# Rounding the weights of an attention and FFN kernel through PSUM, in the score buffers

## The chip, the cores and the metric

The kernel runs on one core of a Trainium2 chip. The metric is the device time of one execution in microseconds, given as the median of several runs. Engines are named as the profile names them: PE (TensorE matmuls), PEld (its weight loads), DVE (VectorE), ACT (ScalarE), POOL (GpSimd), SP (SyncE, which issues most DMAs here). Each engine has a queue of its own.

## What is computed

Two blocks follow each other. Routing attention: queries and keys are each assigned to the nearest of 16 centroids of their head, and a query sees only keys with the same assignment. Then a feed-forward block with a quick GELU. The attention inputs are float32; the two weight matrices arrive as float64 words, and the kernel rounds them to float32 itself, from their integer halves.

```python
batch, n_heads, seq, head_dim = (4, 8, 768, 64); n_clusters = 16
n_tokens, d_model, d_ff = (3072, 512, 2048)
...
q_assign = np.argmax(np.einsum('bhsd,hcd->bhsc', q_n, c_n), axis=-1)
k_assign = np.argmax(np.einsum('bhsd,hcd->bhsc', k_n, c_n), axis=-1)
mask = q_assign[:, :, :, None] == k_assign[:, :, None, :]
scores = scale * np.matmul(q, k.transpose(0, 1, 3, 2))
scores = np.where(mask, scores, -1000000000.0)
...
attn = attn / (np.sum(attn, axis=-1, keepdims=True) + 1e-09)
attn_out = np.matmul(attn, v)
...
x = attn_out.transpose(0, 2, 1, 3).reshape(B * S, H * D)
h = x @ w_in
g = h * (1.0 / (1.0 + np.exp(-1.702 * h)))
return g @ w_out
```

## The kernel before

The work is cut into units. A pair p is two heads of one batch (16 pairs). A group g is one pair and one half of its 768 queries (32 groups), and a unit u is a group and one tile of 128 keys (six to a group, 192 units). A unit's scores are two matmuls into one buffer of the PSUM pool ps_s (L386). For the pairs of batch 0 (p < HP) the mask is added in PSUM by two small matmuls over one-hot codes (part, L400), and the exponential goes to SBUF (L411, tile A). For later pairs the exponential is written back to PSUM and DVE multiplies it by the mask (L422). POOL adds up the exponentials of a group's key tiles (sum, L432), PE multiplies by v (values, L443), and after a group's six tiles `normalise` forms the row sums on PE (L455), takes the reciprocal and the product on DVE (L458, L460), which gives x. `check` (L470, L472) lets ACT sum the reciprocals for a test at the end; its result `bad` decides whether a slower general path is run after all. It is read into every engine by values_load.

The main loop runs over turns t of two units each, and its text is the order of each engine's queue: the schedule is manual. A turn issues the scores, part and exponentials of both units, a step of the weight rounding, the masks and sums, the values of the turn before, `normalise` when a group is done, the preparation of later pairs (prep_turn, prep_near, prep_assign, prep_hot, prep_spread), the check, and then chunks of the FFN. The first turns (t < TB = 24) belong to batch 0. When four groups are normalised, `ffn_chunks` appends 28 chunks: 16 of the first layer (`first`, L489 with tanh L494 and the product L496) and 12 of the second (`second`, L506, L512). The first group of four is complete in turn 13. `rate` chunks are owed per turn, 28 / 11.5 = 2.43. Chunks call `round_to`, which rounds on demand whatever weights they need.

The weights are rounded in 32 pieces of 128 x 512, first w_in's and then w_out's. SP loads a piece into one of three tiles raw (L146). `split_w` takes the exponent and the high mantissa bits (L159, L161 on DVE) and rescales both on ACT (L163, L165). `join_w` puts the sign in (L171), adds the low mantissa word (L174), both on DVE, and multiplies the two parts on POOL (L177). `round_next` splits piece i and joins piece i - 1. It is called once ahead of the loop and once a turn, and twice a turn from t = 12 (TB // 2).

PSUM: ps_s has two buffers of two banks (scores), ps_o one bank (values), ps_m three banks (everything else, the FFN too).

Of the kernel before, what the change touches and what calls it, by code (L numbers as in the profile page):

```python
# [8 lines left out]
FP32 = mybir.dt.float32  # L9
# [29 lines left out]
def fast(  # L39
# [26 lines left out]
    P = 128  # L66
# [74 lines left out]
    w_raw, w_pow = {}, {}  # L141
# [12 lines left out]
    def split_w(i):  # L154

        hi = w_raw[i][:, :, 1]
        w = w_chunks[i][0]
        e = wp.tile([P, WN], I32, name="e")
        nc.vector.tensor_scalar(out=e, in0=hi, scalar1=EXP, scalar2=None,  # L159
                                op0=ALU.bitwise_and)  # L160
        nc.vector.tensor_scalar(out=w.bitcast(I32), in0=hi, scalar1=0xFFFFF,  # L161
                                scalar2=None, op0=ALU.bitwise_and)
        nc.scalar.activation(out=e, in_=e, func=AF.Relu, scale=8.0,  # L163
                             bias=low[:, 0:1])
        nc.scalar.activation(out=w, in_=w.bitcast(I32), func=AF.Copy,  # L165
                             scale=2.0 ** -20, bias=1.0)
        w_pow[i] = e

    def join_w(i):
        raw, e, w = w_raw.pop(i), w_pow.pop(i), w_chunks[i][0]  # L170
        nc.vector.scalar_tensor_tensor(  # L171
            out=e, in0=raw[:, :, 1], scalar=-2 ** 31, in1=e,
            op0=ALU.bitwise_and, op1=ALU.bitwise_or)
        nc.vector.scalar_tensor_tensor(  # L174
            out=w, in0=raw.bitcast(U32)[:, :, 0], scalar=2.0 ** -52, in1=w,
            op0=ALU.mult, op1=ALU.add)
        nc.gpsimd.tensor_tensor(out=w, in0=w, in1=e.bitcast(FP32),  # L177
                                op=ALU.mult)

    w_done = [0]  # L180

    def round_next():
        i = w_done[0]
        if i < NW:
            load_w(i + 2)
            split_w(i)
        if 0 < i <= NW:
            join_w(i - 1)
        w_done[0] += 1

    def round_to(n):
        while w_done[0] <= min(n, NW):
            round_next()
# [333 lines left out]

    prep_at = {}
# [14 lines left out]
    def prep(p, i):  # L543
        if i == 0 and p:
            load_v(p)
        PREP[i](p)
        if i in (1, 3) and loads:
            load_qk(*loads.popleft())

    rate = (NF + NH * (NF // 4)) / (TB / 2 - 0.5)  # L550
# [3 lines left out]
    round_next()  # L554
    for t in range(NT + 2):
        us = range(2 * t, 2 * t + 2) if t < NT else ()
        for u in us:
            scores(u)
        if t == 0:
            prep(0, 6)  # L560
        for u in us:
            part(u)
        for u in us:
            exps(u)
        round_next()
        for u in us:
            mask(u)
        work = sorted(prep_at.get(t, ()), key=lambda w: PREP[w[1]] != prep_near)
        while work and PREP[work[0][1]] == prep_near:
            prep(*work.pop(0))  # L570
        if 1 <= t <= NT:
            for u in range(2 * t - 2, 2 * t):
                values(u)
        owed = owed + rate if ffn else 0.0
        if t >= 2 and (t - 2) % TG == TG - 1:
            normalise((t - 2) // TG)
        for p, i in work:
            prep(p, i)
        if recs:
            check(*recs)  # L580
        if t >= TB // 2:
            round_next()
        while owed >= 1 and ffn:
            ffn.popleft()()
            owed -= 1

# [15 lines left out]
    is_bad = nc.values_load(bad[0:1, 0:1], min_val=0, max_val=1)  # L602
    while ffn:
        ffn.popleft()()
    return is_bad
# [440 lines left out]
```

## Time and profile before

| | |
|---|---|
| median of 3 runs | 1090.87 us (1090.25 to 1093.47) |
| the profiled execution | 1093.03 us, span 1091.2 us |
| mean granted TensorE clock | 0.987 |
| PE busy | 1050.7 us (96%) |
| DVE busy | 484.9 us (44%) |
| ACT busy | 355.2 us (33%) |
| POOL busy | 336.6 us (31%), of it L432 292.8 and L177 43.2 |

The span is the time from the first to the last instruction. Busy shares are means over a span whose stages differ, so the stretches matter more than the means. A row of a timeline gives the start, the duration, the engine, the line and the operation with its operands, and in brackets how long the engine stood idle ahead of it and what ended that. An x with a number is a count of merged instructions; an fp32 matmul of this kernel leaves two records. In the table by stretch each engine's busy time is followed by its count of instructions, and the last three columns are the granted clock (1.00 is full speed), the share of the DMA engines and the GB/s they moved.

### The profile page before, as it was taken

To read this page: it belongs to the slowest core of one execution; us is meant where nothing else is said; L and a number is where in the kernel's file an instruction comes from. 1 tells how busy PE (TensorE), PEld (TensorE's weight loads), DVE (VectorE), ACT (ScalarE), POOL (GpSimd) and SP (SyncE) were. 2 spreads that over 40 slices of the span, in tenths; PEclk is the share of its full clock that TensorE was granted. 3 is DMA by queue.
4 is the path that set the end of the run, shared out by engine and by line. 5 is a ranking of instruction groups with operands and counts; after the bars stand their busy time and mean duration, and the time that the engine had idled before them with its cause. 6 is when DMAs were issued, how large, how long until landed. Compare 5 with 4: busy or idle time off the path is not lost. (4 is left out here: it accounts for less than half of the span.)

```text
span 1091.2 us, 10473 instructions
## 1 busy us (share of the span) xinstructions
PE 1050.7 (96%) x3982; PEld 494.2 (45%) x3982; DVE 484.9 (44%) x712; ACT 355.2 (33%) x665; POOL 336.6 (31%) x200
## 2 busy tenths in 40 slices
PE   6787899999999999999999999999999999999997
PEld 3332454445544455445554455444554445444543
DVE  4889986125442444424443254332553144421100
ACT  5564554233322333223432233322431132311100
POOL 2677646213232333122231243123233233320000
PEclk9898899999999999999999999999999999999999
DMA  8543442110100010101200001020000000000000
GB/s 232 154 127 105 130 112 73 46 49 20 46 23 27 10 29 15 31 25 54 51 22 17 20 15 27 3 70 10 8 8 11 10 11 1 1 10 20 1 10 22
DMA packets 64811, 45.12 MB, mean 41 GB/s; under 512 B 51952, under 2 KB 57584, under 8 KB 64752
## 3 DMA queue, kind: packets, MB, share of 16 engines
q1 hardware_dynamic: 64608, 44.33, 14.5%
q8 instruction: 33, 0.54, 0.2%
q14 instruction: 26, 0.21, 0.1%
q10 hardware_dynamic: 144, 0.03, 0.0%
HBM read 38.04 MB, written 6.31 MB: 41 GB/s over the span
## 5 line engine op out<-in xcount | busy, mean ns | idle before, releaser
L489 PE MATMUL m<-x,w_in 128*128 128x384 f32 x1024 | 346.8, 494 | 7.7 <-DVE g L496 3.1
L432 POOL TENSOR_TENSOR sum<-sum,A 128x768 f32<-128x768 f32 x128 | 234.4, 1831 | 383.5 <-DVE A L422 364.2
L506 PE MATMUL m<-w_out,g 128*128 128x512 f32 x768 | 337.7, 594 | 0.0
L422 DVE SCALAR_TENSOR_TENSOR A<-qb,code,s 128x384 f32<-128x384 uint8 x288 | 157.6, 610 | 274.6 <-ACT s L411 251.5
L489 PEld LDWEIGHTS m<-x,w_in 128*128 128x128 f32 x1024 | 192.3, 192 | 146.8 <-issue 16.0
L506 PEld LDWEIGHTS m<-w_out,g 128*128 128x128 f32 x768 | 143.4, 190 | 174.6 <-issue 171.7
L496 DVE SCALAR_TENSOR_TENSOR g<-g,m 128x384 f32<-128x384 f32 x128 | 70.1, 553 | 228.6 <-ACT g L494 228.4
L386 PE MATMUL s<-T,T 64*128 64x384 f32 x768 | 154.7, 522 | 4.4 <-ACT A L411 4.4
L411 ACT ACTIVATE s<-s 128x768 f32<-128x768 f32 x144 | 107.9, 793 | 136.1 <-PE s L386 136.1
L443 PE MATMUL o<-A,inv 128*64 128x384 f32 x768 | 145.9, 501 | 0.0
L494 ACT ACTIVATE g<-m 128x384 f32<-128x384 f32 x128 | 61.6, 486 | 203.3 <-PE m L489 203.1
L432 POOL TENSOR_TENSOR sum<-A 128x768 f32<-128x768 f32 x32 | 58.4, 1826 | 180.0 <-DVE A L422 179.2
L386 PEld LDWEIGHTS s<-T,T 64*128 64x128 f32 x768 | 67.2, 190 | 87.3 <-issue 52.7
L458 DVE RECIPROCAL short<-m 128x384 f32<-128x384 f32 x32 | 81.7, 2553 | 27.2 <-PE m L455 27.2
L443 PEld LDWEIGHTS o<-A,inv 128*64 128x64 f32 x768 | 46.9, 137 | 85.3 <-issue 85.0
L512 ACT ACTIVATE y<-m 128x512 f32<-128x512 f32 x24 | 14.2, 593 | 155.9 <-PE m L506 142.7
L470 ACT ACTIVATE short<-short 128x384 f32<-128x384 f32 x32 | 16.7, 523 | 103.6 <-DVE x L460 103.6
L411 ACT ACTIVATE A<-s 128x768 f32<-128x768 f32 x48 | 36.4, 808 | 33.0 <-PE s L400 32.8
L269 ACT COPY T<-m 128x384 f32<-128x384 f32 x64 | 29.9, 480 | 41.6 <-PE m L264 41.4
L264 PE MATMUL m<-ident,in 128*128 128x128 f32 x192 | 34.7, 302 | 8.4 <-DVE short L458 3.5
L264 PEld LDWEIGHTS m<-ident,in 128*128 128x128 f32 x192 | 22.0, 149 | 28.1 <-issue 11.1
L177 POOL TENSOR_TENSOR w_in<-w_in,e 128x512 f32<-128x512 f32 x16 | 21.0, 1313 | 42.5 <-DVE w_in L174 42.5
(68 smaller groups left out, 412.4 us busy)
## 6 DMA issues: line engine op xcount, KB each, us to landing
raw<-in_moe_w_in_dram SPq DMA_DIRECT2D x16, 512.0 KB
raw<-in_moe_w_out_dram SPq DMA_DIRECT2D x16, 512.0 KB
in<-in_q_dram SPq DMA_DIRECT2D x32, 192.0 KB
in<-in_k_dram SPq DMA_DIRECT2D x32, 192.0 KB
inv<-in_v_dram SPq DMA_DIRECT2D x16, 384.0 KB
out_dram<-y SPq DMA_DIRECT2D x24, 256.0 KB
qb<-line SPq DMA_DIRECT2D x12, 192.0 KB
line<-row SPq DMA_DIRECT2D x12, 1.5 KB
```

Source lines behind the costliest of these rows:

```text
L264: nc.tensor.transpose(out=ps[:, n * P:(n + 1) * P], in_=qk_in[p, w][:, h * NH + n].rearrange("p a d -> p (a d)"), identity=ident)
L269: nc.scalar.copy(dst, ps[:, 0:HALF])
L386: nc.tensor.matmul(out=ps[:, a, 0:HALF], lhsT=T[p, 1][rows, kt * P:(kt + 1) * P], rhs=T[p, 0][rows, h * HALF:(h + 1) * HALF], start=True, ...
L411: nc.scalar.activation(out=A_of[u] if p < HP else s, in_=s, func=AF.Exp, scale=SCALE)
L422: nc.vector.scalar_tensor_tensor(out=A_of[u][:, a, :], in0=qcode[p][:, a, h * HALF:(h + 1) * HALF], scalar=code[p][:, kt % NH, 1, kt // NH ...
L432: nc.gpsimd.tensor_tensor(out=sum_of[g], in0=A_of[u - 1] if kt == 1 else sum_of[g], in1=A, op=ALU.add)
L443: nc.tensor.matmul(out=o_of[g][a * D:(a + 1) * D, 0:HALF], lhsT=v_in[p][:, a, kt, :], rhs=A[:, a, :], start=(kt == 0), stop=(kt == NJ - 1))
L458: nc.vector.reciprocal(out=rec, in_=ps[:, 0:HALF])
L489: nc.tensor.matmul(out=ps[:, 0:HALF], lhsT=w_in[:, c, f * P:(f + 1) * P], rhs=xT[c], start=(c == 0), stop=(c == NCH - 1))
L494: nc.scalar.activation(out=g, in_=ps[:, 0:HALF], func=AF.Tanh, scale=0.851)
L496: nc.vector.scalar_tensor_tensor(out=g, in0=g, scalar=1.0, in1=ps[:, 0:HALF], op0=ALU.add, op1=ALU.mult)
L506: nc.tensor.matmul(out=ps[:, 0:DM], lhsT=hs[f][:, n * P:(n + 1) * P], rhs=w_out[:, f, :], start=(f == 0), stop=(f == NF - 1))
```

## The change

The multiply that POOL did for each piece moves to DVE. The two rescaled parts are no longer kept in SBUF (e and the weight tile) but in a tile r taken from ps_s, the pool of the score buffers: ACT writes both parts there, and DVE reads them from there, with the result of L174 written to PSUM too. `round_next` becomes `begin` (load, split) and `finish` (join); a piece is begun and finished inside one turn. In the turns of batch 0 the two units of a turn are issued one after the other, with the first piece of the turn begun between them, so that units and pieces alternate in ps_s. Up to t = 11 every fourth turn has no piece; from t = 12 there are two pieces a turn. Until t = 24 the FFN gets 2.1 chunks a turn (SLOW) instead of 2.43. At the end the flag is loaded when four FFN chunks are left, and no longer right after it has been computed with 19 chunks left.

```diff
--- before.py
+++ after.py
@@ -138,7 +138,7 @@
                                  (w_out, moe_w_out, NF, DM))
         for n in range(0, n_n, WN) for c in range(n_c)]
     NW = len(w_chunks)
-    w_raw, w_pow = {}, {}
+    w_raw, w_part = {}, {}
 
     def load_w(i):
         if i < NW:
@@ -153,44 +153,51 @@
 
     def split_w(i):
 
         hi = w_raw[i][:, :, 1]
         w = w_chunks[i][0]
-        e = wp.tile([P, WN], I32, name="e")
+        e = wp.tile([P, WN], I32, name="e", bufs=2)
+        r = ps_s.tile([P, 2, WN], FP32, name="s")
         nc.vector.tensor_scalar(out=e, in0=hi, scalar1=EXP, scalar2=None,
                                 op0=ALU.bitwise_and)
         nc.vector.tensor_scalar(out=w.bitcast(I32), in0=hi, scalar1=0xFFFFF,
                                 scalar2=None, op0=ALU.bitwise_and)
-        nc.scalar.activation(out=e, in_=e, func=AF.Relu, scale=8.0,
-                             bias=low[:, 0:1])
-        nc.scalar.activation(out=w, in_=w.bitcast(I32), func=AF.Copy,
+        nc.scalar.activation(out=r.bitcast(I32)[:, 0, :], in_=e, func=AF.Relu,
+                             scale=8.0, bias=low[:, 0:1])
+        nc.scalar.activation(out=r[:, 1, :], in_=w.bitcast(I32), func=AF.Copy,
                              scale=2.0 ** -20, bias=1.0)
-        w_pow[i] = e
+        w_part[i] = e, r
 
     def join_w(i):
-        raw, e, w = w_raw.pop(i), w_pow.pop(i), w_chunks[i][0]
+        raw, (e, r), w = w_raw.pop(i), w_part.pop(i), w_chunks[i][0]
         nc.vector.scalar_tensor_tensor(
-            out=e, in0=raw[:, :, 1], scalar=-2 ** 31, in1=e,
+            out=e, in0=raw[:, :, 1], scalar=-2 ** 31,
+            in1=r.bitcast(I32)[:, 0, :],
             op0=ALU.bitwise_and, op1=ALU.bitwise_or)
         nc.vector.scalar_tensor_tensor(
-            out=w, in0=raw.bitcast(U32)[:, :, 0], scalar=2.0 ** -52, in1=w,
-            op0=ALU.mult, op1=ALU.add)
-        nc.gpsimd.tensor_tensor(out=w, in0=w, in1=e.bitcast(FP32),
+            out=r[:, 1, :], in0=raw.bitcast(U32)[:, :, 0], scalar=2.0 ** -52,
+            in1=r[:, 1, :], op0=ALU.mult, op1=ALU.add)
+        nc.vector.tensor_tensor(out=w, in0=r[:, 1, :], in1=e.bitcast(FP32),
                                 op=ALU.mult)
 
-    w_done = [0]
-
-    def round_next():
-        i = w_done[0]
+    w_at = [0, 0]
+    def begin():
+        i = w_at[0]
         if i < NW:
             load_w(i + 2)
             split_w(i)
-        if 0 < i <= NW:
-            join_w(i - 1)
-        w_done[0] += 1
+            w_at[0] += 1
+    def finish():
+        if w_at[1] < w_at[0]:
+            join_w(w_at[1])
+            w_at[1] += 1
 
     def round_to(n):
-        while w_done[0] <= min(n, NW):
-            round_next()
+        while w_at[1] < min(n, NW):
+            begin()
+            finish()
 
     load_qk(1, 0)
     load_v(0)
@@ -525,6 +532,9 @@
     TG = NJ // 2
     TB = 2 * HP * TG
 
+    RATE = (NF + NH * (NF // 4)) / (TB / 2 - 0.5)
+    SLOW = 2.1
     prep_at = {}
     for p in range(1, NPAIR):
         b, hp = divmod(p, HP)
@@ -547,42 +557,51 @@
         if i in (1, 3) and loads:
             load_qk(*loads.popleft())
 
-    rate = (NF + NH * (NF // 4)) / (TB / 2 - 0.5)
     owed = 0.0
     for p, i in [(0, i) for i in range(6)] + [(1, i) for i in range(2)]:
         prep(p, i)
-    round_next()
+    begin()
+    finish()
     for t in range(NT + 2):
-        us = range(2 * t, 2 * t + 2) if t < NT else ()
-        for u in us:
-            scores(u)
-        if t == 0:
-            prep(0, 6)
-        for u in us:
-            part(u)
-        for u in us:
-            exps(u)
-        round_next()
-        for u in us:
-            mask(u)
+        us = list(range(2 * t, 2 * t + 2)) if t < NT else []
+        n = 1 if t < TB else 2
         work = sorted(prep_at.get(t, ()), key=lambda w: PREP[w[1]] != prep_near)
-        while work and PREP[work[0][1]] == prep_near:
-            prep(*work.pop(0))
-        if 1 <= t <= NT:
-            for u in range(2 * t - 2, 2 * t):
-                values(u)
-        owed = owed + rate if ffn else 0.0
-        if t >= 2 and (t - 2) % TG == TG - 1:
-            normalise((t - 2) // TG)
+        for late, part_us in enumerate((us[:n], us[n:])):
+            for u in part_us:
+                scores(u)
+            if t == 0 and not late:
+                prep(0, 6)
+            for u in part_us:
+                part(u)
+            for u in part_us:
+                exps(u)
+            for u in part_us:
+                mask(u)
+            if late:
+                continue
+            if t % 4 != 3 or t >= TB // 2:
+                begin()
+            while work and PREP[work[0][1]] == prep_near:
+                prep(*work.pop(0))
+            if 1 <= t <= NT:
+                for u in range(2 * t - 2, 2 * t):
+                    values(u)
+            owed = owed + (RATE if t >= TB else SLOW) if ffn else 0.0
+            if t >= 2 and (t - 2) % TG == TG - 1:
+                normalise((t - 2) // TG)
+        finish()
         for p, i in work:
             prep(p, i)
         if recs:
             check(*recs)
         if t >= TB // 2:
-            round_next()
+            begin()
         while owed >= 1 and ffn:
             ffn.popleft()()
             owed -= 1
+        finish()
 
 
     ok = const.tile([P, 2, 2 * NPAIR], FP32, name="ok")
@@ -599,9 +618,10 @@
     bad = const.tile([1, 1], I32, name="bad")
     nc.vector.tensor_scalar(out=bad, in0=okt, scalar1=-1.0, scalar2=1.0,
                             op0=ALU.mult, op1=ALU.add)
-    is_bad = nc.values_load(bad[0:1, 0:1], min_val=0, max_val=1)
     while ffn:
         ffn.popleft()()
+        if len(ffn) == 4:
+            is_bad = nc.values_load(bad[0:1, 0:1], min_val=0, max_val=1)
     return is_bad
```

## The prediction

> **What bounds the kernel now.** I first read the table by stage, which cuts the span into stretches with each engine's busy time and the granted TensorE clock.
>
> ```profile
> 20.00:40.00 20.00, 16.63 (x104) 7.39 (x103) 16.87 (x21) 11.48 (x21) 12.35 (x8) 0.91 0.64 176
> 60.00:80.00 20.00, 18.09 (x120) 7.90 (x120) 18.67 (x23) 13.91 (x25) 13.16 (x8) 1.00 0.36 102
> 80.00:100.00 20.00, 14.21 (x65) 4.90 (x65) 19.83 (x20) 10.07 (x19) 15.33 (x10) 0.83 0.37 112
> 100.00:150.00 50.00, 43.86 (x172) 21.09 (x174) 47.19 (x55) 26.57 (x50) 31.09 (x21) 0.93 0.42 122
> 300.00:400.00 100.00, 100.00 (x358) 45.68 (x357) 40.85 (x60) 28.49 (x56) 30.02 (x17) 1.00 0.07 20
> ```
>
> The first number after the length is PE, the third DVE. From 150 us on PE has no gap worth naming (100.00 of 100 here; 0.9 idle from 150 to 250). Before that it waits, and from 60 to 108 us DVE is 93 to 99% busy. So the span is PE's work plus what PE loses: 29.6 us idle up to 150, the same stretch's matmuls at a clock of 0.83 to 0.93, and 7.9 us in the last stretch. Nothing else in the change can pay.
>
> The timeline of DVE and POOL shows why DVE is full, and that of PE what it loses:
>
> ```profile
> 91.17 1.49 DVE L161 TENSOR_SCALAR w_in<-raw 128x512 int32<-128x512 int32 x1
> 92.58 2.30 DVE L171 SCALAR_TENSOR_TENSOR e<-raw,e 128x512 int32<-128x512 int32 x1
> 94.80 2.29 DVE L174 SCALAR_TENSOR_TENSOR w_in<-raw,w_in 128x512 f32<-128x512 uint32 x1
> ...
> 92.33 4.21 POOL L432 TENSOR_TENSOR sum<-sum,A 128x768 f32<-128x768 f32 x2
> ...
> 299.29 3.70 POOL L432 TENSOR_TENSOR sum<-sum,A 128x768 f32<-128x768 f32 x2 [8.64 <-DVE A L422]
> 299.59 0.60 DVE L422 SCALAR_TENSOR_TENSOR A<-qb,code,s 128x384 f32<-128x384 uint8 x1
> ```
>
> L171 and L174 take 0.68 us alone and 2.30 when POOL is summing: they end when a sum ends. L422, which reads one operand from PSUM, takes 0.60 in the middle of a sum; over all its runs it stays within 605 to 617 ns, L496 (also one PSUM operand) within 540 to 556.
>
> ```profile
> 103.69 2.20 PE L489 MATMUL m<-x,w_in 128*128 128x384 f32 x6
> 108.20 3.49 PE L489 MATMUL m<-x,w_in 128*128 128x384 f32 x10 [2.31 <-DVE x L460]
> 112.13 1.61 PE L386 MATMUL s<-T,T 64*128 64x384 f32 x8 [0.43 <-ACT A L411]
> 115.54 2.85 PE L489 MATMUL m<-x,w_in 128*128 128x384 f32 x8
> 121.52 5.49 PE L489 MATMUL m<-x,w_in 128*128 128x384 f32 x8 [3.13 <-DVE g L496]
> 1021.88 0.27 PE L596 MATMUL m<-ident,ok 128*1 128x128 f32 x1
> 1024.11 19.99 PE L489 MATMUL m<-x,w_in 128*128 128x384 f32 x56 [1.96 <-DVE bad L600]
> ```
>
> The first FFN chunk waits for x (L460) until 108.2. Then PE waits for DVE again, and after the gap the same eight records take 5.49 instead of 2.85. At 1022 it waits for the flag.
>
> **A, the Vector queue up to x (gain 12.3 us).** Line numbers are those of the kernel before. In the order of the changed program, 13 splits (L159, L161) and 12 joins (L171, L174 and the new multiply) stand ahead of the reciprocal and product of head group 3; before it was 16 and 15. Removed: three pieces at their start-to-start steps, 3 x (0.34 + 0.33 + 0.60 + 0.60) = 5.6; the joins' waits for POOL, which between 16 and 108 us are eight runs over 0.68 (seven of about 2.30, one of 1.17), 11.8 together; and the share of three pieces in the splits' waits (11.3 over 16 pieces, so 2.1). Added: 12 multiplies. The trace has none with a PSUM operand and 512 columns. The bounds: 0.60 per step, as L171 and L174 without a wait; 0.74, L496's 0.554 scaled to 512 columns. I take 0.60, because L496's 0.154 beyond its columns (384 at 0.96 per ns, 0.40) is nearly L171's 0.147 beyond its 0.533: 12 x 0.60 = 7.2. At the other end all 36 join steps cost 0.14 more, 5.0 us. Sum: 5.6 + 11.8 + 2.1 - 7.2 = 12.3, so x is ready at 95.9 instead of 108.2. The lock on the splits stays (9.2 us of waits): they still read and write SBUF alone.
>
> [...] The two rows just compared show 7 ns, so the sum keeps 12.3.
>
> The loop through the shared buffers does not bind here: scores 0.75 and part 0.21, exponential 0.70, L163 and L165 1.24, then two DVE steps 1.28, after which the next turn's scores may start: 4.2 us, against (95.9 - 16.2) / 13 = 6.1 a turn. POOL loses its products of 1.27 (L177), so its sums only get earlier. The 11.5 us that DVE idles between 16 and 108 are kept. Join 0 now stands ahead of pair 0's copy L356, which comes some 2 us later, and so does the first part; the wait for raw at 21.85 covers that, and without it A would be 10. SP issues the same loads in nearly the same order, each behind a join that is earlier; waits of DVE for raw were 7.5 us in all, 5.4 of them at 21.85, and stay.
>
> **B, what PE gives back at once (7.3 us).** In turn 14 the FFN stands in PE's queue behind the second unit's scores, and these now wait until the first unit's exponential has left their buffer. On ScalarE that exponential stands behind L163 and L165 of piece 13, whose split follows join 12: 95.9 + 1.8 (join) + 0.35 + 1.2 (two activations) + 0.75 (exponential) + 1.1 (scores, part, hand-off) = 101.1. Before, the FFN resumed at 108.2 with six of its sixteen records done, 2.1 us. The lead on PE is 108.2 - 2.1 - 101.1 = 5.0 us, not 12.3.
>
> **C, what before then lost (gain 6.2).** 0.43 + 3.13 idle and 5.49 - 2.85 = 2.64 slow. In the new order turn 15's chunks find their banks free: the products of turn 14 (L496) come out by 108.6 on DVE (two activations of piece 15, two tanh, two products after 104.4), and PE asks for the bank at about 110.
>
> **D, turns 16 to 23 (cost 4.4).** With two pieces a turn, DVE needs 2 x (0.34 + 0.33 + 1.80) = 4.94, 2.1 products of 0.47 = 1.0, and a third of a reciprocal and product (2.6 + 0.5), 1.0: 7.0. It stands idle for ScalarE about 0.4 ahead of the first join and 1.45 ahead of L496 (two activations and two tanh), 8.8; the second unit's sum catches one split operation a turn, 1.2: 10.0. PE needs 1.5 + 0.43 + 1.44 for attention, 0.6 for preparation and sums, 2.1 x 2.58 = 5.4 for the FFN: 9.4. So 0.6 over the five turns with first-layer chunks is 3.0; second-layer chunks (3.44 each) cover the rest. Also: at 2.1 chunks a turn the last two first-layer chunks fall in turn 21, after the copy of group 6 into the x buffer that they read. That copy (L448, 0.48) then waits on ScalarE for them, with the second exponential (0.75) and L163, L165 behind it, and PE's next scores wait for this: 1.4. The lock on the split, if it catches both sums each turn, is rival 2. The FFN's lag of some three chunks costs nothing: PE is busy 100.00 of 100 us later on, and does them there.
>
> **E, the flag's load near the end (gain 3.1).** Now: 1.96 idle, and the granted clock is 0.78, 0.50 and 0.93 in the three stretches from 1024 to 1032, worth 0.44 + 1.0 + 0.28 = 1.7. Together 3.7. Four chunks before the end the flag is long there. The load's own time is between 0 and the 0.59 from the flag's end (1023.52) to the next matmul; I charge 0.6. Gaps of 0.57 at 234.3 left the clock at 1.00 in that stretch.
>
> **Sum.** 5.0 + 6.2 - 4.4 + 3.1 = 9.9 us off the profiled execution: 1093.0 (span 1091.2, 1.8 around it) becomes 1083.1. The median of the runs is 0.998 of that execution, so 1081.
>
> **Rivals.** (1) More: the splits' waits, 9.2 left in A, halve because POOL has fewer operations and each piece's split now starts while the first sum has not begun (4.6), and D's chain hides (3.0): 17.5 off, 1073. For it: no product on POOL delays a sum. Against: sums alone caused most of the 2.03 us runs. (2) Slower: the loop of turns 12 to 22, in which scores use one buffer and pieces the other, becomes the bound: if both sums each catch a split (2.8 instead of 1.2), a turn is 11.6, 2.2 over PE's 9.4, for eight turns 17.6 instead of 3.0: 4.7 over before, 1095. It decides from 11.0 a turn. For it: before's turns from 111.28 to 184.42 took 10.4. Against: their joins waited too. (3) The change does not do what it says: operations with a PSUM operand and one from SBUF wait for POOL as well. Then A's 11.8 is gone and the sum is 1.9 over before, 1093. Against: L422 and L496 never do; for it: neither writes PSUM, as the new L174 does.
>
> **How the numbers follow.** Forecast 0.52 (its own range 1076 to 1087), rival 1 0.20, rival 2 0.17, rival 3 0.11. The range runs from 1070 (rival 1 with the whole of the splits' rest near gone) to 1093 (rival 3; with the dearer PSUM step the forecast ends at 1086). A measurement of this kernel tells some 0.3%, 3.3 us, from no change. Faster: forecast, rival 1 and a little of 3, 0.76; same 0.08; slower, rival 2 and part of 3, 0.16.
>
> **What would show it.** The three join operations at 0.67 to 0.75 us with no run of 2.3 during a sum; POOL with 32 fewer instructions, about 43 us less; first FFN matmuls near 101; no PE gap of 3 us with half-speed records near 120; turns of 9.4 to 10.5 from 16 to 22; a gap under 1 us at the flag. Wrong: join operations of 2.3 (rival 3), turns over 11 (rival 2), or PE gaps before 100 longer than now.

## The result, and the profile after

The changed kernel takes 1122.03 us (1121.19 to 1123.34) where the kernel before took 1090.73 us beside it: a ratio of 1.0283, 95% interval 1.0263 to 1.0303. It is 31 us slower; the forecast was 10 us faster, and the time lies 29 us above the range. Line numbers of the changed kernel are seven higher from the exponential on (x is L467, FFN L496, scores L393); the split is L161, L163, its activations L165, L167, the join L173, L177 and, for the new multiply, L180.

The table by stage of the changed kernel, with PE first, DVE third and the granted clock after the five engines:

```profile
60.00:80.00 20.00, 18.04 (x112) 7.34 (x114) 13.62 (x18) 12.66 (x23) 9.33 (x5) 0.93 0.47 130
80.00:100.00 20.00, 16.98 (x80) 5.76 (x80) 15.29 (x22) 10.71 (x20) 9.61 (x6) 0.85 0.36 104
...
150.00:200.00 50.00, 43.08 (x180) 20.05 (x179) 36.17 (x57) 25.75 (x46) 12.67 (x7) 0.97 0.36 111
200.00:250.00 50.00, 45.52 (x149) 19.92 (x150) 22.73 (x35) 15.45 (x28) 10.93 (x6) 0.93 0.16 47
300.00:400.00 100.00, 100.00 (x369) 46.27 (x367) 41.34 (x64) 28.13 (x54) 27.12 (x15) 1.00 0.07 18
```

DVE is relieved: 13.62 of 20 us between 60 and 80, where it had 18.67, and 15.29 between 80 and 100 instead of 19.83. PE gets nothing from it. Between 150 and 250 us, where it was all but full before (0.9 us idle), it now stands 11.4 us (50 - 43.08 and 50 - 45.52). From 300 us on it is full as before, so the loss is made in the first 250 us.

The busy time from 16 us to the end of x of head group 3 (the product that opens the FFN) makes this exact. First the kernel before, then the changed one:

```profile
16.00:108.20 92.20, 73.64 (x429) 31.32 (x426) 79.49 (x89) 53.83 (x97) 61.87 (x38) 0.91 0.50 143
```

```profile
16.00:116.20 100.20, 77.05 (x407) 30.08 (x407) 70.92 (x93) 53.31 (x91) 41.93 (x23) 0.85 0.40 116
```

DVE did the same stage with 8.6 us less work (79.49 to 70.92) and took 8.0 us longer. Its idle time went from 12.7 (92.20 - 79.49) to 29.3 us. The list of waits names the reason. Its rows give who waited, for whom, the total in us, how often, and the longest. Up to x, the kernel before and then the changed one:

```profile
DVE e L171 <- ACT e L163: 2.2, 1, 2.2
```

```profile
DVE e L173 <- ACT s L167: 22.4, 10, 5.1
```

DVE waited 22.4 us, ten times, for L167, the second activation of a piece; before, it waited 2.2 us, once. The timeline of turn 6, all engines, shows one such wait:

```profile
64.17 0.42 DVE L161 TENSOR_SCALAR e<-raw 128x512 int32<-128x512 int32 x1
...
64.57 0.92 PE L393 MATMUL s<-T,T 64*128 64x384 f32 x4
...
65.85 0.81 ACT L418 ACTIVATE A<-s 128x768 f32<-128x768 f32 x1 [0.36 <-PE s L407]
66.56 0.69 ACT L165 ACTIVATE s<-e,low 128x512 int32<-128x512 int32 x1
67.28 0.60 ACT L167 ACTIVATE s<-w_in 128x512 f32<-128x512 int32 x1
...
67.91 0.69 DVE L173 SCALAR_TENSOR_TENSOR e<-raw,s 128x512 int32<-128x512 int32 x1 [2.99 <-ACT s L167]
68.64 0.69 DVE L177 SCALAR_TENSOR_TENSOR s<-raw,s 128x512 f32<-128x512 uint32 x1
69.36 0.69 DVE L180 TENSOR_TENSOR w_in<-s,e 128x512 f32<-128x512 f32 x1
...
70.11 0.59 PE L393 MATMUL s<-T,T 64*128 64x384 f32 x2 [0.21 <-DVE w_in L180]
```

The split was done by 64.9. Its activations stand on ACT behind the first unit's exponential, which waits for its scores, so they begin at 66.56. The join needs both and stands next in DVE's queue: DVE is idle for 2.99 us. The next turn's scores take the piece's buffer only when L180 has read it. From the scores at 64.57 to those at 70.11 it is 5.54 us in a turn that nothing else disturbs.

The join itself does what was foretold. DVE's and POOL's timelines near 88 and 99 us:

```profile
88.39 1.81 POOL L439 TENSOR_TENSOR sum<-A 128x768 f32<-128x768 f32 x1 [1.85 <-ACT A L418]
99.44 1.82 POOL L439 TENSOR_TENSOR sum<-sum,A 128x768 f32<-128x768 f32 x1 [2.64 <-ACT A L418]
```

```profile
88.53 0.69 DVE L180 TENSOR_TENSOR w_in<-s,e 128x512 f32<-128x512 f32 x1
99.52 2.03 DVE L163 TENSOR_SCALAR w_in<-raw 128x512 int32<-128x512 int32 x1
```

L180, with one operand in PSUM, takes 0.69 in the middle of a sum, and so it is throughout. The split L163, which has none, takes 2.03 there instead of 0.42; it ends 0.29 us after the sum.

PE's timeline where the FFN should have opened:

```profile
118.41 1.65 PE L393 MATMUL s<-T,T 64*128 64x384 f32 x4 [6.10 <-DVE w_in L180]
...
124.37 0.91 PE L496 MATMUL m<-x,w_in 128*128 128x384 f32 x2
```

x ended at 116.2, the join that stood behind it freed the scores' buffer at 118.3 (PE idle 6.10), and the first chunk ran at 124.37, where 101.1 was foretold and the kernel before had its first at 103.69. At the end, PE goes from the flag's transpose (1052.30) to FFN matmuls at 1052.41 without a gap.

### The profile page after: what moved, and what is told of

Its sections match the earlier page's. It is cut to its first block, busy times and chain, and to the rows that moved or that the text cites. A ratio compares the mean times of both kernels' runs of the same rounds, so it can differ in the third digit from the quotient of the medians.

```text
span 1120.4 us, 10534 instructions
## 1 busy us (share of the span) xinstructions
PE 1065.4 (95%) x3982; PEld 495.6 (44%) x3982; DVE 487.1 (43%) x744; ACT 359.6 (32%) x665; POOL 291.2 (26%) x168
## 5 line engine op out<-in xcount | busy, mean ns | idle before, releaser
L439 POOL TENSOR_TENSOR sum<-sum,A 128x768 f32<-128x768 f32 x128 | 231.9, 1812 | 465.0 <-DVE A L429 367.8
L496 PE MATMUL m<-x,w_in 128*128 128x384 f32 x1024 | 343.5, 491 | 1.5 <-DVE x L467 1.2
L496 PEld LDWEIGHTS m<-x,w_in 128*128 128x128 f32 x1024 | 191.3, 191 | 137.0 <-issue 11.5
L393 PE MATMUL s<-T,T 64*128 64x384 f32 x768 | 160.2, 525 | 24.0 <-DVE w_out L180 10.8
L450 PE MATMUL o<-A,inv 128*64 128x384 f32 x768 | 150.9, 516 | 0.0
L393 PEld LDWEIGHTS s<-T,T 64*128 64x128 f32 x768 | 65.3, 189 | 113.1 <-issue 56.8
L418 ACT ACTIVATE A<-s 128x768 f32<-128x768 f32 x48 | 38.7, 807 | 31.6 <-PE s L407 31.4
L271 PE MATMUL m<-ident,in 128*128 128x128 f32 x192 | 35.3, 307 | 11.4 <-DVE short L465 3.9
L276 ACT COPY T<-m 128x384 f32<-128x384 f32 x64 | 30.0, 480 | 38.4 <-PE m L271 38.2
L165 ACT ACTIVATE s<-e,low 128x512 int32<-128x512 int32 x32 | 22.1, 690 | 49.9 <-DVE e L161 49.9
L173 DVE SCALAR_TENSOR_TENSOR e<-raw,s 128x512 int32<-128x512 int32 x32 | 21.9, 684 | 31.2 <-ACT s L167 31.2
```

The source lines that it names most:

```text
L271: nc.tensor.transpose(out=ps[:, n * P:(n + 1) * P], in_=qk_in[p, w][:, h * NH + n].rearrange("p a d -> p (a d)"), identity=ident)
L276: nc.scalar.copy(dst, ps[:, 0:HALF])
L393: nc.tensor.matmul(out=ps[:, a, 0:HALF], lhsT=T[p, 1][rows, kt * P:(kt + 1) * P], rhs=T[p, 0][rows, h * HALF:(h + 1) * HALF], start=True, ...
L418: nc.scalar.activation(out=A_of[u] if p < HP else s, in_=s, func=AF.Exp, scale=SCALE)
L439: nc.gpsimd.tensor_tensor(out=sum_of[g], in0=A_of[u - 1] if kt == 1 else sum_of[g], in1=A, op=ALU.add)
L450: nc.tensor.matmul(out=o_of[g][a * D:(a + 1) * D, 0:HALF], lhsT=v_in[p][:, a, kt, :], rhs=A[:, a, :], start=(kt == 0), stop=(kt == NJ - 1))
```

## The experiments

Each figure is the median beside runs of the kernel before on the same chip, with the ratio to it and its interval. Medians of the kernel before were 1090.3 to 1090.8.

**First set: is it the sharing of buffers?** e1_flag is the kernel before with the late load of the flag:

```diff
-    is_bad = nc.values_load(bad[0:1, 0:1], ...)
     while ffn:
         ffn.popleft()()
+        if len(ffn) == 4:
+            is_bad = nc.values_load(bad[0:1, 0:1], ...)
```

> The kernel before with one part of the change alone: the flag is loaded when four FFN chunks are left. If step E of the prediction holds, 3.1 us less than before (1090.7 to about 1087.6), with the PE gap of 1.96 us near the flag under 1 us and the granted clock there at 1.00. If the load itself drains PE wherever it stands, 0 to 1 us less.

Measured 1088.38, ratio 0.9970 (0.9959 to 0.9981): 3.3 us off (2.1 to 4.5). Its timeline of PE after the flag:

```profile
1021.21 0.27 PE L596 MATMUL m<-ident,ok 128*1 128x128 f32 x1
1021.32 18.23 PE L489 MATMUL m<-x,w_in 128*128 128x384 f32 x56
```

Before, the same 56 records waited 1.96 us and took 19.99. The granted clock is 1.00 in the stretch after it.

e2_sbuf is the changed kernel with the pieces' parts in SBUF, everything else as changed:

```diff
-        r = ps_s.tile([P, 2, WN], FP32, name="s")
...
-        nc.scalar.activation(out=r.bitcast(I32)[:, 0, :], in_=e, func=AF.Relu, ...)
-        nc.scalar.activation(out=r[:, 1, :], in_=w.bitcast(I32), func=AF.Copy, ...)
+        nc.scalar.activation(out=e, in_=e, func=AF.Relu, ...)
+        nc.scalar.activation(out=w, in_=w.bitcast(I32), func=AF.Copy, ...)
```

> The changed kernel with the two rescaled parts of a piece kept in SBUF, as before, and the multiply still on DVE; order, rates and flag as changed. Theory 1 (serial loop through the shared buffers: the next scores wait for a join on DVE, the join for ScalarE): the scores no longer wait for joins, so 15 to 25 of the 31 us come back, 1097 to 1107. Theory 2 (DVE has too much in its queue): the joins wait for POOL again and DVE gets fuller, 1125 to 1140.

Measured 1119.40, ratio 1.0247 (1.0225 to 1.0268), between the ranges of the two theories. Only some 3 us of the loss go with the sharing. Its row up to x, in the order as above:

```profile
16.00:116.10 100.10, 81.46 (x425) 31.61 (x424) 77.41 (x91) 51.48 (x90) 43.12 (x23) 0.84 0.39 114
```

x ends at 116.1, as in the changed kernel. With parts in SBUF DVE is busy 6.5 us more (77.41 against 70.92: the joins wait for POOL again) and idle 6.6 us less (22.7 against 29.3). So the immunity of the joins is real, 6.5 us of busy time here where step A counted 11.8, and all of it comes back as idle time.

e3_two is the changed kernel with both units of a turn issued together (`n = 2` in place of `n = 1 if t < TB else 2`):

> The changed kernel with both units of a turn issued together in batch 0 too, ahead of the piece; pieces still in the score buffers. If the second exponential standing behind the piece's two activations is the main loss, 1100 to 1108. If the buffers are (theory 1), both units of the next turn now wait for the joins and it stays at 1115 to 1130.

Measured 1156.71, ratio 1.0589 (1.0568 to 1.0610), far above both ranges. The list of PE's waits up to 250 us shows where the buffers are held:

```profile
PE s L393 <- DVE w_in L180: 35.0, 11, 5.4
PE s L393 <- DVE w_out L180: 21.2, 7, 4.0
```

e4_rate is the changed kernel with 2.43 FFN chunks a turn instead of 2.1 (`SLOW = RATE`):

> The changed kernel with 2.43 instead of 2.1 FFN chunks a turn in batch 0. If PE's idle time in turns 14 to 23 (about 11 us between 112 and 226 us) is a loop that does not include the FFN, the 3.3 chunks brought forward fill it and the time falls by up to 9 us, to 1113. If the FFN's products on DVE are in that loop, within 3 us of 1122 or longer.

Measured 1119.22, ratio 1.0249 (1.0229 to 1.0270): some 3 us better, not the main loss.

**Second set: single parts of the new order.** e5_mul is the kernel before with the pieces' multiply on VectorE:

```diff
-        nc.gpsimd.tensor_tensor(out=w, in0=w, in1=e.bitcast(FP32),
+        nc.vector.tensor_tensor(out=w, in0=w, in1=e.bitcast(FP32),
                                 op=ALU.mult)
```

> Kernel before with one edit: the last multiply of each piece on VectorE instead of GpSimd (parts stay in SBUF, the join a turn behind its split, both units together). Theory M (the moved multiply loads the engine that bounds the early stage): 12 multiplies at 0.7 us land before x of head group 3, so x comes 5 to 8 us later and the time is 1097 to 1103. Theory J (the loss of the change comes from the join standing in the turn of its split): the multiply fills waits that the joins had behind GpSimd, 1086 to 1094. Theory U (the loss comes from the two units of a turn issued one after the other): the same 1086 to 1094.

Measured 1103.06, ratio 1.0111 (1.0092 to 1.0129). x ends at 119.5 instead of 108.2, and DVE is busy 88.0 us up to there instead of 79.5. Where DVE is the bound, theory M holds; x comes 11.3 us later where it named 5 to 8.

e7_inturn is the kernel before with the join moved to the end of the turn of its own split:

```diff
-        round_next()
+        begin()
         for u in us:
             mask(u)
...
             normalise((t - 2) // TG)
+        finish()
...
         if t >= TB // 2:
-            round_next()
+            begin()
         while owed >= 1 and ffn:
             ...
+        finish()
```

> Kernel before with one edit: the join of a piece stands at the end of the turn of its split, where the change puts it (multiply on GpSimd, parts in SBUF, both units together, one piece a turn and then two). Theory J: the join's first step now waits for the two activations of its own piece, ScalarE's activations wait for the split, and the preparation's VectorE work stands behind the join; x of head group 3 comes 6 to 12 us later and the time is 1105 to 1118. Theory U: 1088 to 1095. Theory M: 1088 to 1095.

Measured 1112.09, ratio 1.0188 (1.0169 to 1.0207), as theory J had it. DVE waits 13.1 us for L163 up to x (before 2.2), and x ends at 123.2. But the edit does two things: the join comes in the turn of its split, and it comes later within the turn. The fifth set prices the second by itself.

e8_late is e2_sbuf with each join one piece behind its split:

```diff
     def finish():
-        if w_at[1] < w_at[0]:
+        if w_at[1] < w_at[0] - (w_at[0] < NW):
```

> The changed kernel with its parts in SBUF and each join one piece behind its split, as before the change; it keeps the multiply on VectorE, the units one after the other, three pieces in four turns, the rate of 2.1 and the late flag load. Theory J: most of the loss is gone, 1086 to 1097. Theory U: the loss stays, 1112 to 1120. Theory M: the loss stays, 1110 to 1120.

Measured 1111.58, ratio 1.0183 (1.0165 to 1.0202): 7 to 8 us back, and x at 109.2, but 20 us of loss stay. Theory J is right for x and wrong as the whole cause.

e9_units is the kernel before with the units of batch 0 one after the other and the piece's step between them:

```diff
+        for late, part_us in enumerate((us[:n], us[n:])):
+            for u in part_us:
+                scores(u)
             ...
+            for u in part_us:
+                mask(u)
+            if late:
+                continue
+            round_next()
             ...
```

> Kernel before with one edit: in the first batch the two units of a turn are issued one after the other, the piece's step and the other work between them, as in the change (multiply on GpSimd, parts in SBUF, join a turn behind, one piece a turn). Theory U: the second unit's exponential stands behind the piece's activations and its scores behind the first unit's values; 1105 to 1118. Theory J: 1088 to 1096. Theory M: 1088 to 1096.

Measured 1102.95, ratio 1.0095 (1.0067 to 1.0123), a loss of 7 to 13 us, between the ranges. This edit too does more than its name says: the piece's multiply on POOL now stands behind the first unit's sum. Three single edits cost 10 to 21 us each; they add to more than the whole, so their costs overlap.

**Third set: crosses.** e6_sbuf_two is the changed kernel with parts in SBUF and units together:

> The changed kernel with the pieces' parts in SBUF and both units of a turn issued together (join in the turn of its split, multiply on VectorE, three pieces in four turns, rate 2.1, late flag load). It stands against the same order with the parts in the scores' buffers (1156.7) and against the units one after the other with the parts in SBUF (1119.4). If the three edits cost separately what they cost in the kernel before (multiply 12.4, join in the turn 21.5, one unit after the other 12.3), taking the last away gives 1105 to 1112. If the sharing of buffers is what made units together bad, the time lies below 1125 in any case. If the units together with a join in the same turn are bad in themselves, it is 1145 to 1158.

Measured 1124.96, ratio 1.0314 (1.0289 to 1.0340). At the 1125 named as the limit for the sharing, too close to decide by that number (its four runs lie between 1120.58 and 1126.40), but well over the 1105 to 1112 of separate costs and well under the 1145 for units together being bad in themselves. Sharing costs 32 us with the units together (1156.71 against this) and some 3 us with the units alternating (1122.03 against 1119.40). The alternation is what makes the sharing bearable.

e10_three_flag is e1_flag with three pieces in four turns up to turn 11:

```diff
-        round_next()
+        if t % 4 != 3 or t >= TB // 2:
+            round_next()
```

> Kernel before with two parts of the change only: three pieces in four turns up to turn 11 (and so more pieces later), and the late flag load, which alone gave 1088.4. If fewer pieces relieve the engine that bounds the early stage, as step A had it (5.6 us for three pieces), 1080 to 1086. If the pieces are only put off into turns 12 to 23, where they cost as much, 1087 to 1092.

Measured 1089.11, ratio 0.9982 (0.9968 to 0.9996): no gain over e1_flag. But x ends at 100.5, 7.7 us earlier. The table by stage shows where that is given back, and PE's waits in 150 to 200 us by what:

```profile
190.00:200.00 10.00, 5.11 (x9) 1.80 (x8) 5.83 (x8) 3.13 (x8) 3.50 (x3) 0.81 0.21 61
```

```profile
PE m L506 <- POOL w_out L177: 4.9, 2, 3.5
```

The FFN's second layer catches up with the pieces and forces the last ones: PE is busy 5.11 of 10 us and its clock falls to 0.81.

e11_start is the changed kernel with the first join moved behind the first copy of the hot rows:

```diff
     begin()
-    finish()
     for t in range(NT + 2):
         ...
                 prep(0, 6)
+                finish()
```

> The changed kernel with the join of the first piece moved behind the copy of the first hot rows in turn 0, where the kernel before has no join at all. If the 6.5 us by which the scores of turn 1 are late stay up to the end, 1115 to 1119. If the turns behind it are paced by the pieces' own chain and swallow the start, 1120 to 1123.

Measured 1120.64, ratio 1.0267 (1.0242 to 1.0292). x ends at 116.5 as before the edit (116.2): the late start is swallowed.

e12_xbuf is the changed kernel with seven x tiles instead of six (`bufs=HP + 3`):

> The changed kernel with one more buffer for the x tiles (7 instead of 6), which takes away ScalarE's two waits for the FFN's matmuls before it copies x, 7.6 us in the trace. If they are on the path (step D put 1.4 on them), 1114 to 1120.5. If they lie beside other work, 1121 to 1123.

Measured 1118.16, ratio 1.0249 (1.0224 to 1.0274): about 4 us, where step D had 1.4.

**Fourth set: undoing part by part.** e13_ladder is e8_late with the multiply back on GpSimd; e14_ladder2 is that with the units together again.

```diff
-        nc.vector.tensor_tensor(out=w, in0=w, in1=e.bitcast(FP32),
+        nc.gpsimd.tensor_tensor(out=w, in0=w, in1=e.bitcast(FP32),
...
-        n = 1 if t < TB else 2
+        n = 2
```

> The changed kernel with parts in SBUF and the join one piece behind its split (together 1111.6), and the multiply back on GpSimd; units one after the other, three pieces in four turns, rate 2.1 and the late flag load stay. If the multiply costs here what it cost by itself in the kernel before (12.4), 1097 to 1101. If its price was that of a full VectorE, which three pieces in four turns relieve, 1105 to 1111.

> The one before with both units of a turn issued together again; what is left of the change is three pieces in four turns, rate 2.1, the late flag load and the place of the piece's step within the turn. Three pieces with the late flag alone gave 1089.1, the rate cost 2.8 in the changed kernel: 1089 to 1094 if the three parts undone are the whole loss. If something else of the new order costs, above 1096.

Measured 1110.37, ratio 1.0185 (1.0165 to 1.0206), and 1110.57, ratio 1.0162 (1.0129 to 1.0195; its four runs lie between 1102.37 and 1111.72, so this figure is the least certain). Neither edit moves the time by more than its uncertainty. Every part that I had named was undone, and 18 us of loss stood.

e15_catch is e10_three_flag with a third piece in turns 15, 17 and 19; e16_catch2 has two pieces in three turns up to turn 11 and a third one in turns 15 to 18.

```diff
         if t >= TB // 2:
             round_next()
+        if t in (15, 17, 19):
+            round_next()
```

> Kernel before with the late flag load, three pieces in four turns up to turn 11, and the three pieces so put off made up as a third piece in turns 15, 17 and 19. Without these the trace had the first FFN matmul 5.5 us earlier (98.2 against 103.7) and the last pieces forced by the FFN at 190 to 202 us, with 4.9 us of TensorE idle, a granted clock of 0.81 and no VectorE idle. If step A's relief by fewer pieces is real and was only given back there, 1081 to 1086. If VectorE in turns 15 to 19 has no room for them, 1088 to 1093.

> The same idea one step further: two pieces in three turns up to turn 11, a third piece in each of turns 15 to 18, late flag load. If VectorE's queue up to x of head group 3 still sets the start of the FFN, another 1 to 3 us off the one before. If PE's own chain through the scores and exponentials sets it by now, the same as the one before within 1 us, or up to 4 more where turns 15 to 18 have no room.

Measured 1086.29, ratio 0.9965 (0.9952 to 0.9978), and 1087.49, ratio 0.9974 (0.9962 to 0.9986). e15's median is 2.8 us under e10's, just above what step A's relief was expected to give. In e16 x comes earlier still, at 98.9, without gain.

**Fifth set: what the ladder had left over.** e17_rate is e10_three_flag with 2.1 chunks a turn up to turn 23; e18_place is e14_ladder2 with 2.43 chunks and the split ahead of the masks, meant to leave of the new places only that of the join.

```diff
-        owed = owed + rate if ffn else 0.0
+        owed = owed + (rate if t >= TB else 2.1) if ffn else 0.0
```

```diff
             for u in part_us:
                 exps(u)
+            if not late and (t % 4 != 3 or t >= TB // 2):
+                begin()
             for u in part_us:
                 mask(u)
...
-            if t % 4 != 3 or t >= TB // 2:
-                begin()
```

> Three pieces in four turns and the late flag load in the kernel before (1089.1), with the change's rate of 2.1 FFN chunks a turn up to turn 23. What is left between this and the kernel at the end of the ladder (1110.6) is then only the place of the piece's steps within the turn. If the place is what costs, 1089 to 1093; if the rate is, 1105 to 1111.

> The kernel at the end of the ladder (1110.6; units together, multiply on GpSimd, join a piece behind, parts in SBUF) with the rate of before and the split where the kernel before has it, ahead of the masks; the join alone stays at the end of the turn, behind the values and the normalisation (and behind the FFN chunks from turn 12 on). If the join's place costs, 1100 to 1110; if it was the split's place or the rate, 1087 to 1094.

Measured 1083.60, ratio 0.9933 (0.9908 to 0.9958), below both of its ranges, and 1102.36, ratio 1.0099 (1.0072 to 1.0127), as for the join's place. e17 is faster than the kernel before, and its median is the lowest here. Against e14_ladder2 (1110.57) it differs only in where within the turn the split and the join stand; a few lines moved cost 25 us by the ratios.

The traces show that it is the join alone. In batch 0 a split gives POOL nothing to do and a mask gives work to POOL only, so moving the split past the masks reorders no engine's queue: up to 140 us e18_place and e14_ladder2 run the same operations in the same order on PE, DVE, ACT and POOL, and behind that only the rate of the FFN's chunks sets them apart. e17_rate and e14_ladder2, and likewise e10_three_flag and e18_place, have one order on PE and on ACT from start to end. What differs is the join: on DVE it moves behind the reciprocal and product, and from turn 12 on the second one behind the FFN's products; on POOL its multiply moves behind the sums. So the join's place costs 13 us at 2.43 chunks a turn (e10 to e18) and 25 to 27 us at 2.1 (e17 to e14). The lower rate gains 5 us with the early join (e10 to e17) and costs 7 to 8 us with the late one (e18 to e14, with the reserve named above for e14).

The path from the best kernel to the changed one, one edit a row. "x" is the end of x of head group 3; "turn 24" is the start of that turn's scores, read from PE's timeline:

| kernel | adds | us | ratio | x | turn 24 |
|---|---|---|---|---|---|
| e17_rate | three in four, rate 2.1, late flag | 1083.60 | 0.9933 | 101.9 | 203.0 |
| e14_ladder2 | the join's place in the turn | 1110.57 | 1.0162 | 111.4 | 230.3 |
| e13_ladder | units one after the other | 1110.37 | 1.0185 | 109.7 | 228.8 |
| e8_late | multiply on DVE | 1111.58 | 1.0183 | 109.2 | 230.5 |
| e2_sbuf | join in the turn of its split | 1119.40 | 1.0247 | 116.1 | 239.6 |
| changed | parts in the scores' buffers | 1122.03 | 1.0283 | 116.2 | 240.8 |

All six run 2.1 chunks a turn up to here, so the start of turn 24 can be compared: 37.8 us from first to last row, against 38.4 in the medians. Everything is lost by then, 14 us of it up to x and 24 in the ten turns after it. Two of the rows are large, the place and the join's turn; 13 us for the place at the other rate and 7 to 8 us for the turn add up to about what e7_inturn lost with both (20.5 us by its ratio). The rows hold for this order of the edits: with the parts in the scores' buffers, units together cost 35 us (e3_two), and here nothing. Differences of 2 us in the column x say nothing, since e18_place, in the same order up to there as e14_ladder2, has x at 109.8.

What the place does after x can be read from DVE's groups by shape, each with its count, its busy time, the mean ns of one and the idle time ahead of it. First e17_rate, from its x to its turn 24 (102 to 203 us), then e14_ladder2 (111.4 to 230.3), where the split is L160 and L162, the join on DVE L172 and L176, the tanh L500 and the FFN's product L502:

```profile
L159 DVE TENSOR_SCALAR e<-raw 128x512 int32<-128x512 int32 x19 | 20.3, 1066 | 2.5 <-DMA raw<-in_moe_w_out_dram 1.9 <-DMA raw<-in_moe_w_in_dram 0.6
L171 DVE SCALAR_TENSOR_TENSOR e<-raw,e 128x512 int32<-128x512 int32 x20 | 18.5, 923 | 0.0
L161 DVE TENSOR_SCALAR w_out<-raw 128x512 int32<-128x512 int32 x16 | 13.1, 819 | 0.0
...
L496 DVE SCALAR_TENSOR_TENSOR g<-g,m 128x384 f32<-128x384 f32 x16 | 8.1, 543 | 0.4
```

```profile
L172 DVE SCALAR_TENSOR_TENSOR e<-raw,e 128x512 int32<-128x512 int32 x21 | 24.0, 1144 | 0.0
L162 DVE TENSOR_SCALAR w_out<-raw 128x512 int32<-128x512 int32 x16 | 22.8, 1428 | 0.0
...
L160 DVE TENSOR_SCALAR e<-raw 128x512 int32<-128x512 int32 x19 | 8.5, 447 | 0.6 <-DMA raw<-in_moe_w_in_dram 0.6
L502 DVE SCALAR_TENSOR_TENSOR g<-g,m 128x384 f32<-128x384 f32 x16 | 8.2, 551 | 8.9 <-ACT g L500 8.9
```

The splits cost the same in both. In e17_rate their waits for POOL fall on the first operation (1066 ns, where e14_ladder2 has 447), in e14_ladder2 on the second (1428 against 819); with the three pieces of w_in the 19 splits take 37.3 and 36.3 us. Two other things differ. A join's two operations on DVE take 2.03 us on average instead of 1.66 (42.6 us for 21 and 33.2 for 20). And DVE stands idle 8.9 us instead of 0.4 for ACT's tanh ahead of the FFN's product. One such wait in e14_ladder2:

```profile
155.09 1.50 DVE L162 TENSOR_SCALAR w_out<-raw 128x512 int32<-128x512 int32 x1
...
157.66 1.02 DVE L502 SCALAR_TENSOR_TENSOR g<-g,m 128x384 f32<-128x384 f32 x2 [1.07 <-ACT g L500]
...
158.27 5.43 PE L495 MATMUL m<-x,w_in 128*128 128x384 f32 x16 [1.97 <-DVE g L502]
```

The split's second operation takes 1.50 us beside the multiply that the join ahead of it had just given to POOL (from 154.91, 1.39 us); the split's activation on ACT, the tanh behind that and the product on DVE follow in a chain, and PE waits for the product. In e17_rate a join of 1.2 us or more stands on DVE between the split and the product and fills that time. PE waits 8.7 us for this product in e14_ladder2 and 3.5 in e17_rate. Up to x it is the splits that get longer (18.9 us for 23 operations, 23.1 for 22), the joins a little (24.9 for 24 operations, 27.0 for 23), and the preparation waits 12.2 us for PE instead of 8.8. These are the rows that differ; no run separates the join's place on DVE from that of its multiply on POOL.

## Why the prediction was wrong

**The step that failed is A**, in the sentence "The 11.5 us that DVE idles between 16 and 108 are kept". A counted DVE's work ahead of x, and took x to move with it, from 108.2 to 95.9; it ended at 116.2. Of that work, most was right. Three pieces fewer were 5.6 us; in e10_three_flag, e15_catch and e17_rate x ends 7.7, 6.1 and 6.2 us earlier. The join operations never wait for POOL (means of 685 to 696 ns). DVE's busy time up to x fell by 8.6 us, against 12.3. But DVE's idle time was not kept; it rose by 16.6 us, from 12.7 to 29.3, and 22.4 of that is the join's wait for ACT.

The check that should have caught this was that of the loop. It was priced at 4.2 us and took 5.54 undisturbed, above all because it ended after two steps of the join, 1.28, where the third, the multiply, reads the same buffer: the three take 2.20 (67.91 to 70.11). Comparing it with 6.1 a turn was wrong in kind: other DVE work stands between one turn's join and the next split, so the idle time inside the turn adds to that work; it doesn't run beside it. The buffers themselves matter little here: without the sharing (e2_sbuf) x still ends at 116.1. Before, a split was followed by the join of the piece before, whose activations were done but for one wait of 2.2 us up to x. I wrote down that join and split now share a turn, and A charged nothing for it. e8_late to e2_sbuf puts 7 to 8 us on it, nearly all before x.

**The join's place in the turn had no price in the sum at all.** It is the largest term (25 to 27 us at the change's rate, e17_rate to e14_ladder2). I counted what stands ahead of x in DVE's queue, 13 splits and 12 joins, and not between which operations of POOL and ACT they land.

**The term of 0.60 us for each multiply and join step** was the lower end of its bounds. Measured from start to start: 0.72 (L173 to L177, mostly), 0.73 (L177 to L180), 0.61 to the next; 12 pieces x (2.06 - 1.80) = 3.1 us, where the sum had nothing. The 0.96 columns per ns behind my choice are what the kernel before shows between 128 x 64 and 128 x 384: 220 and 553 ns for a reduction (L229, L295), 226 and 558 for a product (L228 and the shortest L460), 320 columns in 333 and 332 ns. The two rows 7 ns apart were durations, and in these the changed join differs little too (medians of 686 and 696 ns, where L171 and L174 have 684 and 680); its cost lies between the starts. But only about half of the 3.1 us goes with PSUM. With the parts in SBUF and the multiply on DVE (e2_sbuf, e5_mul, e8_late) the steps are 0.60, 0.72 and 0.61: the multiply, which reads what the operation ahead of it has just written, starts 0.72 behind it there too.

**B and C** rested on x at 95.9 and fall with it. PE's gap in turn 14 is longer than before, 6.10 us, now behind join 13.

**D** had turns of 10.0 us; from turn 16 (139.65) to 24 (240.81) they took 12.6, 21 us more in the eight turns. It failed as A did: DVE's work was to set the turn, and DVE was busy only 66.5 of these 101.2 us. Rival 2 saw the stage and the size better (11.6, and slower), at 0.17. Its cause was only in part the right one: PE's waits for w_out's multiply are there (10.8 us, eight times), but without sharing e2_sbuf takes 123.5 us from x to turn 24, against 124.6. The x-buffer wait was foreseen, at turn 21, and mis-sized: 1.4 against some 4.

**E** was right: 3.1 forecast, 3.3 by the ratio of e1_flag.

**Rival 1** had the splits' waits for POOL right and nothing else: up to x they fell from 11.3 to 4.4 us, where A kept 9.2. Other operations took part of that over (the product of `normalise` and the hot rows, 6.1 us before and 10.6 after), and none of it brought x forward. **Rival 3** can be ruled out by the rows of 0.69 us during a sum. **The cover of the first join** was none, turn 1's scores began at 23.53 instead of 17.02, but e11_start shows that it costs 1 to 2 us at most.

## What to carry to other kernels

DVE, 93 to 99% busy from 60 us to x in the kernel before, was not a queue whose length alone set the end: with 8.6 us less work it took 8.0 us longer. If an edit moves an operation to another place in a turn, ask for each of its inputs which engine makes it, what stands ahead of it there, and whether it is old or fresh when the queue gets to it; a result asked for in the turn that starts it was paid here as 22.4 us of idle time in the very engine that was relieved. Relief of one stage was kept only where the deferred work had room later: three pieces in four turns gave nothing until the pieces put off were made up sooner (1089.11 to 1086.29) or the consumer was slowed (1083.60). And an edit of the text is an edit of the schedule only where it changes the order of some engine's queue (e14_ladder2 and e18_place, in one order up to 140 us, have x at 111.4 and 109.8): compare the queues before putting a time down to a moved line.

## What was not expected of the hardware

A DVE operation of 128 x 512 with one PSUM operand takes about as long as from SBUF (685 to 696 ns against 0.68 us). What PSUM costs shows in one step of the join, from its first to its second operation: 0.71 to 0.79 us from start to start, where the same step from SBUF is 0.60 to 0.62 (e2_sbuf). The next step, in which the multiply reads the result just written, is 0.73 from PSUM and 0.72 from SBUF.

The operations that wait for POOL wait elsewhere when the order changes, and not always more: the mean of the split's second operation went from 819 to 1428 ns between e17_rate and e14_ladder2, and that of its first from 1066 to 447.

The rate of 2.1 chunks has opposite signs in different kernels: it costs some 3 us in the changed one (e4_rate) and 7 to 8 with the late join (e18_place to e14_ladder2), and in e10_three_flag it gains 5.5 (e17_rate).
